# Ties for the loads of w2, h2T and w1 to products, a third output buffer, and a lower pace of the first stages, in a fused spectral-gate and MLP step

## The chip, the core and the metric

The kernel runs on one core of a Trainium2 chip. The metric is device time in microseconds, taken as the median of repeated executions. The engines are TensorE (PE, matmul), VectorE (DVE), ScalarE (ACT), GpSimd (POOL) and SyncE (SP). In this kernel SP issues nearly all loads and every transposing load, in one queue and in order; GpSimd issues nearly all stores and a few loads. Matmuls read weights and streams from the on-chip memory (SBUF) and add up in PSUM banks, from which ScalarE or VectorE take them.

## What is computed

A gated sum of two branches, and then all its gradients for a given `grad_out`. Cut to what matters:

```python
X = rfft2(x) * (w_r + 1j * w_i)                # x: 2048 x 1024
a = irfft2(X, s=(2048, 1024)).astype(bfloat16) # branch A
h = x @ w1 + b1                                # w1: 1024 x 3584
r = where(h > 0, h, 0)
b = (r * r) @ w2 + b2                          # branch B, w2: 3584 x 1024
g = sigmoid((x * gate_w).sum(-1, keepdims=True))
out = g * a + (1 - g) * b
# returned: out, and its vjp at grad_out for
# x (through both branches and the gate), w_r, w_i, w1, b1, w2, b2 and gate_w
```

The large matrix products are: h (hidden), its gradient (dh), the gradients of w2 (h transposed times the output gradient) and of w1 (x transposed times dh), the output of branch B (h times w2), and the product of dh with w1 turned (the gradient of x through B). In the kernel the output gradient already times (1-g) is `dbn`, its transpose `dbT`.

## The kernel before

One chain of products on TensorE runs from start to end, and a second, smaller chain, the two Fourier transforms, is threaded into it.

**The main chain** has three stages. `mlp_in` makes h (line 724) and its gradient (line 734) in *units* of two products each, 128 features by 512 rows, and stores the squared activations and the gradients to two scratch tensors in HBM, `h2T_scr` and `dhT_scr`. The pre-activation passes through ScalarE, the gradient through VectorE (line 738). w2 is read by transposing loads `load_w2` into `w2T`, two for each group of 512 features.

`mlp_grads` makes the gradients of w2 and w1 in 28 *blocks*. Each group of 512 features is fetched back from scratch by four transposing loads (`fetch`, line 180) into one of two tiles called "odd" and "even", and serves two blocks. A block is one level of a fast 2 x 2 multiplication: seven products `p1` to `p7` in place of eight, with sums of quarter matrices as operands. For w2 (blocks 0 to 13, lines 913 and following) the sums of the group are S1 to S4 (`left`, line 887), and those of `dbn` are T1 to T4 (`right`, lines 861 to 870), made once at the start of the stage. For w1 (blocks 14 to 27, `Turned`, line 978) the sums of x (`sums_of_x`, line 1006) are made once, and those of each group (`sums_of_group`, line 1023, G1 to G4) for every group. Products accumulate in PSUM banks `pX` and `pV`. ScalarE copies what is needed between products (line 920, `c` and `u`), VectorE adds it up (line 924, `wlo` and `whi`), and GpSimd stores the block. `p7` ends in such an addition, kept as `added`.

`mlp_out` makes branch B's output, `out`, and then the product of dh with w1. h blocks 0 and 1 (256 rows each) are done as eight full products (line 1419), the rest as blocks of seven products (line 1324). Its operands are w2 in two halves, `w2L` (in the place of `dbn`, free after block 13) and `w2R`; three large sums of them, `wT` (line 1384, 3.89 us each) must be made on VectorE before block 2's later products, and each block has its own sums `dS` (line 1320). `prepare` (lines 1241, 1242), `close` (1253, 1254, 1259) and `put` (1263) finish an output tile from `a` (branch A, from `ax_scr`), `go` (the given gradient) and the products. The quarters of w1 for the last products come by transposing loads (`quarter`), two columns of chunks at a time.

**The side chain** has four stages: the row and column transforms of x and of grad_out (`first_stage_of_x`, `first_stage_of_grad`, lines 276 and 309; each tile is fetched by `source` at line 632, folded on VectorE, and stored to `z_scr`); `fft_mid`, 32 turns over `z_scr` which transform along the rows, multiply with the filter, form the filter's gradients and transform back (products `px`, line 415, and `pv`, line 446; VectorE's result `pc`, stored to `y_scr`, lines 452 to 455); and `fft_out`, the transforms back. For a tile, `fft_out` loads rows `r` from `y_scr` on GpSimd's queue (line 225), copies and folds them on ScalarE (line 552) and VectorE (lines 557, 558, `folded`), multiplies (line 565, `rows_back`, and `columns_back`), combines on VectorE (lines 581 to 593, result `yo`) and stores `yo` to `ax_scr` (line 594).

**What sets the order.** Both chains are generators. `spread` advances the side chain by a given number of steps for each unit of the main chain. In `mlp_in` that number is `first_rate`: 2.1 steps a unit until `fft_mid` starts (the flag "mid"), 1.6 after it, none in the last six units. In `mlp_grads`, a product has weight 0.5; the rate is 0.9 a weight until the sums of x are handed on (flag "res1", after block 13's products), and from then the steps left, `todo` less those done, over 48. `fft_out` issues its first three loads of `r` and yields eight times before the first `folded`. The emitted order is then turned by a scheduler into the order on each engine; each engine runs its own instructions strictly in order. `after(ins, earlier)` adds a dependency by hand: by default a wait, or, where it says NoSync, only an order. `turn["PE"]` is the last product issued so far in the order written by hand.

**Which loads stand where.** `rows_of_w2` (line 616) loads four row blocks of one half of w2, 512 KB. In `mlp_grads` seven such loads fill `w2L`, emitted at the ends of the blocks from number 16 on; nothing but the place being free makes them wait. `load` in `mlp_out` (line 1223) fetches a block of h2T or dhT in two loads of 896 KB; block 1 goes to "odd3", a tile of its own, so nothing holds it back either. Each piece of `quarter` waits only for its destination being free. All of these stand in SP's queue with the transposing loads of the groups.

Of the kernel before, what the change touches and what calls it, by code (L numbers as in the profile page):

```python
# [10 lines left out]
P = 128  # L11
# [6 lines left out]
FDT = FP16  # L18
# [121 lines left out]
def kernel(  # L140
# [27 lines left out]
    S, D = xf.shape  # L168
# [3 lines left out]
    R1, R2 = g.R1, g.R2  # L172
    NT = S // P
    Q, H, LW, W1 = D // 4, D // 2, g.Df + 1, g.Df
# [5 lines left out]
    turned = lambda out, in_: nc.sync.dma_start(out=out, in_=in_, transpose=True)  # L180
    ld, st = nc.sync.dma_start, nc.gpsimd.dma_start
# [16 lines left out]
    pers, _ = pool("pers", stack=ctx)  # L198
    dram, _ = pool("dram", space=DRAM, stack=ctx)
# [33 lines left out]
    def after(ins, earlier, wait=mybir.DependencyClass.Sync):  # L233

        if earlier is not None:
            info = mybir.DependencyInfo(wait, mybir.DependencyReason.DATA)
            tc.add_manual_dep(ins.ins, earlier.ins.name, info, reason="paced")


    turn = {"PE": None, "DVE": None, "ACT": None}  # L240
# [288 lines left out]
    def fft_out():  # L529
        odd_p, later["odd_s"] = pool("odd3", "right")  # L530
        later["odd3"] = odd_p.tile([P, FC * 2 * P], BF16, name="odd3", tag="odd3")
        fb, fbs = pool("f3", "right")
        ki = fb.tile([P, 2, P], FDT, name="ki", tag="ki")
        ld(out=ki[:], in_=cten["ki"].ap())
        ci = fb.tile(list(consts["ci"].shape), FDT, name="ci", tag="ci")
        ld(out=ci[:], in_=cten["ci"].ap())
        tiles = [(T, i) for T in range(2) for i in range(NT)]
        r, fold, rt, evens = {}, {}, {}, {}

        def load(n):  # L540
            T, i = tiles[n]
            r[n] = fb.tile([P, D], FDT, name="r", tag="r", bufs=4)
            rows_of(st, y_scr, T, i, r[n], False)

        def folded(n):

            fold[n] = fb.tile([P, 2, 2, P], FDT, name="rf", tag="rf", bufs=2)
            rv = r[n][:].rearrange("p (c h g i) -> p c h g i", c=2, h=2, g=4)
            a, b = rv[:, :, 0, 1::2, :], rv[:, :, 1, 3::-2, ::-1]
            evens[n] = fb.tile([P, 2, 2, P], FDT, name="re", tag="re", bufs=2)  # L550
            for im in range(2):
                nc.scalar.copy(  # L552
                    out=evens[n][:, im].rearrange("p g (h i) -> p g h i", h=2),
                    in_=rv[:, im, :, 0::2, :].rearrange("p h g i -> p g h i"),
                )
            to = lambda sign: fold[n][:, sign].rearrange("p c (g i) -> p c g i", g=2)
            in_turn(V(out=to(0), in0=a, in1=b, op=ALU.add), "DVE")
            in_turn(V(out=to(1), in0=a, in1=b, op=ALU.subtract), "DVE")

        def rows_back(n):  # L560
            pk = fps.tile([P, 8, P], FP32, name="pki", tag="ps2", bufs=2)
            even = [evens[n][:, im, g_] for im, g_ in ((1, 0), (0, 0), (0, 1), (1, 1))]
            odd = [fold[n][:, sign, im] for sign, im in ((0, 0), (1, 0), (1, 1), (0, 1))]
            for b, block in enumerate(even + odd):
                in_turn(mm(pk[:, b, :], lhsT=block, rhs=ki[:, int(b in (1, 2, 4, 5)), :], start=True, stop=True), "PE")
            rt[n] = fb.tile([P, 8, P], FDT, name="rt", tag="rt", bufs=2)
            nc.scalar.copy(out=rt[n][:], in_=pk[:])

        def columns_back(n):
            T, i = tiles[n]  # L570
            pu = fps.tile([P, 2, H], FP32, name="pui", tag="ps2", bufs=2)
            column_stage(pu, rt[n], ci, turn["PE"])
            e = fb.tile([P, 2, H], FDT, name="e", tag="e", bufs=2)
            nc.scalar.copy(out=e[:, 0, :], in_=pu[:, 0, :])
            nc.scalar.copy(
                out=e[:, 1, :].rearrange("p (c d x) -> p c d x", c=2, x=2),
                in_=pu[:, 1, :].rearrange("p (c x d) -> p c d x", c=2, x=2),
            )
            ev = fb.tile([P, 2, Q], FDT, name="ev", tag="ev", bufs=2)
            A, B = (e[:, 0, o : o + Q].rearrange("p (c d) -> p c d", c=2) for o in (0, Q))  # L580
            in_turn(V(out=ev[:, :, 0:P], in0=A, in1=B, op=ALU.add), "DVE")
            evf = ev[:].rearrange("p c d -> p (c d)")
            in_turn(V(out=evf[:, Q:P:-1], in0=A[:, 0, :], in1=B[:, 0, :], op=ALU.subtract), "DVE")
            in_turn(V(out=evf[:, 2 * Q - 1 : Q + P : -1], in0=B[:, 1, 1:], in1=A[:, 1, 1:], op=ALU.subtract), "DVE")
            in_turn(nc.vector.tensor_copy(out=ev[:, :, P : P + 1], in_=e[:, 0, P::Q].rearrange("p (c o) -> p c o", o=1)), "DVE")
            tt = fb.tile([P, 2, 2, Q], FDT, name="tt", tag="tt", bufs=2)
            V(out=tt[:, 0].rearrange("p a b -> p (a b)"), in0=evf, in1=e[:, 1, :], op=ALU.add)
            V(out=tt[:, 1].rearrange("p a b -> p (a b)"), in0=evf, in1=e[:, 1, :], op=ALU.subtract)
            yo = fb.tile([P, D], FDT, name="yo", tag="yo", bufs=2)
            yv = yo[:].rearrange("p (a l) -> p a l", a=2)  # L590
            V(out=yv[:, :, 0:Q], in0=tt[:, :, 0, :], in1=tt[:, :, 1, :], op=ALU.add)
            V(out=yv[:, ::-1, H - 1 : Q : -1], in0=tt[:, :, 0, 1:Q], in1=tt[:, :, 1, 1:Q], op=ALU.subtract)
            nc.vector.tensor_copy(out=yo[:, 0::Q], in_=tt[:, :, :, 0].rearrange("p a b -> p (a b)"))
            st(out=ax_scr[T][i][:], in_=yo[:])

        load(0), load(1), load(2)
        for _ in range(8):
            yield
        folded(0)
        for n in range(len(tiles) + 1):  # L600
            if n < len(tiles):
                rows_back(n)
                yield
            if n > 0:
                columns_back(n - 1)
            if n + 3 < len(tiles):
                load(n + 3)
            if n + 1 < len(tiles):
                folded(n + 1)
            yield  # L610
        fbs.close()


    def rows_of_w2(t_, fc, half):
        src = B_w2[fc * P : (fc + 4) * P, half * H : (half + 1) * H]
        ld(out=t_[:, fc : fc + 4, :], in_=src.rearrange("(q p) e -> p q e", p=P))

    db_p, db_s = pool("db")
    dbn = db_p.tile([P, NT, D], BF16, name="dbn", tag="dbn")
# [4 lines left out]
    later = {}  # L624
# [184 lines left out]
    def mlp_grads():  # L809
# [255 lines left out]
        for k in range(2, NB // 2):  # L1065
            a = blk.pop(k - 1)
            g, second = divmod(k, 2)
            b = blk[k] = Block(k)
# [72 lines left out]
        for k in range(NB // 2 + 2, NB):  # L1141
            g, second = divmod(k, 2)
            b = Turned(k)
            b.p1()
            yield each
            b.p2()
            if second:
                fetch(g + 2, 0)
            yield each
            a.p4()  # L1150
            if not second:
                sums_of_group(g, 3, 4)
            yield each
            b.p6()
            yield each
            a.p3()
            if not second:
                fetch(g + 1, 1)
            yield each
            b.p5()  # L1160
            yield each
            b.p7()
            if second and g + 1 < len(jobs):
                sums_of_group(g + 1, 1, 2, tie=b.added)
            yield each
            n = k - NB // 2 - 2
            if n < FC // 4:
                rows_of_w2(later["w2L"], 4 * n, 0)
            a = b
        a.p4()  # L1170
        yield each
        a.p3()
# [5 lines left out]
    BW = 2 * P  # L1178
# [13 lines left out]
    def mlp_out():  # L1192
# [23 lines left out]
            after(ins, turn["DVE"], mybir.DependencyClass.NoSync)  # L1216
            turn["DVE"] = ins

        def load(which, k, issue=ld):
            t_ = later["odd" if k % 2 else "even"][:, 0 : FC * BW].rearrange("p (c b) -> p c b", b=BW)  # L1220
            v_ = (h2T_scr if which == "h" else dhT_scr)[:].rearrange("c p s -> p c s")
            for h in (lo, hi):
                issue(out=t_[:, h, :], in_=v_[:, h, k * BW : (k + 1) * BW])
            blks[which, k] = t_


# [159 lines left out]
        def quarter(view, i, j):  # L1386
            for c in range(0, KH, 2):
                f0 = (i * KH + c) * P
                turned(view[:, c : c + 2, :], B_w1[j * H : (j + 1) * H, f0 : f0 + 2 * P])
                yield  # L1390


# [15 lines left out]
        prepare(0)  # L1408
        fetch_g(1)
        made = w2_sums()  # L1410
        load("h", 1)
        for fc in range(0, FC, 4):
            rows_of_w2(cR, fc, 1)
        steps = [(0, 0), (1, 0), (2, 0), (0, 1), (1, 1), (2, 1), (3, 0), (3, 1)]
# [294 lines left out]

    def first_rate():  # L1710
        left_[0] -= 1
        return 0.0 if left_[0] < 6 else 1.6 if "mid" in later else 2.1

    for _ in spread(units, spec, first_rate):
        pass
    grads = mlp_grads()
    next(grads), next(grads)
    todo = 22 + 2 * (NT + 4) + 14 + 5 + 4 * R1 + 2 + 8 + 2 * 28

    def rate():  # L1720
        if "res1" not in later:
# [52 lines left out]
```

## Time and profile before

Thirteen executions gave a median of 1254.54 us, 1245.82 to 1264.34. One execution was profiled.

| what | us |
|---|---|
| profiled execution, its time | 1251.89 |
| its span, first to last instruction | 1250.1 |
| TensorE busy | 1196.5 |
| VectorE, ScalarE, GpSimd busy | 831.6, 619.6, 362.6 |
| first products of the two first side stages (line 276), from | 33.6 |
| `fft_mid`'s forward products (line 415), first and last start | 284.9 to 663.0 |
| last unit's products (line 734) start | 471.4 |
| gradient blocks of w2 and w1 | 474.0 to 882 |
| `fft_out`'s products (line 565), first and last start | 714.3 to 894.4 |
| full products of h blocks 0 and 1 (line 1419) | to 932 |
| blocks of seven products (line 1324), from | 932.7 |

How to read the lines of the profile in what follows. A line of a timeline gives the start, the duration in microseconds (from the first to the end of the last where several equal instructions stand together), the engine, the line of the kernel, the operation, the result and its operands, the shapes, the count and, in brackets, how long the engine sat idle before it and what released it. A line of the view of waits gives the engine and the instruction that waited, what it waited for, and then the total in microseconds, the number of waits and the longest. The row PEclk gives, for 40 slices of the span, the clock granted to TensorE in tenths of the full one, where 9 is 0.9 or more. SPq is SP's DMA queue; its duration is the time to issue, not to land.

### The profile page before, as it was taken

The page shows a single profiled execution, that of the slowest core. Times are in us where ns is not written, and L with a number is a line of the kernel's source. Part 1 is how long each engine was busy: PE and PEld are TensorE (multiplying, and loading weights), DVE is VectorE, ACT ScalarE, POOL GpSimd, SP SyncE. Part 2 cuts the span into 40 slices and gives each one's busy share as a digit, 9 for nine tenths or more (in the row PEclk, how much of TensorE's full clock was granted, in tenths as well). Part 3 has the DMA queues.
Part 4 walks back from the last instruction along what each step waited for, and adds up shares of the span by engine and source line. Part 5 has one row for each costly group of instructions (what it writes and reads, how often), then busy time and mean ns, then how long its engine had stood idle before and what let it go on. Part 6 is the DMA issues. An engine that isn't in the chain of part 4 may idle for free. (4 is left out here: it accounts for less than half of the span.)

```text
span 1250.1 us, 20093 instructions
## 1 busy us (share of the span) xinstructions
PE 1196.5 (96%) x7231; PEld 657.3 (53%) x7328; DVE 831.6 (67%) x1808; ACT 619.6 (50%) x1128; POOL 362.6 (29%) x587
## 2 busy tenths in 40 slices
PE   9999998999999998999999599999997999999997
PEld 5555554444444443444447499999543444444443
DVE  3556476768888867776788177777357665875464
ACT  4658686557777763444433166666321323233232
POOL 0124354225555532333234444653100000000000
PEclk9999999999999998999999799999998999999999
DMA  9566576575769699689979999985895558856450
GB/s 284 193 188 183 168 180 208 126 202 176 194 192 232 150 211 178 156 170 232 242 177 229 198 188 192 236 186 173 216 245 141 156 173 200 209 182 201 142 157 34
DMA packets 332382, 234.44 MB, mean 188 GB/s; under 512 B 197772, under 2 KB 291114, under 8 KB 332282
## 3 DMA queue, kind: packets, MB, share of 16 engines
q1 hardware_dynamic: 301856, 142.50, 53.0%
q0 software_dynamic: 30224, 90.61, 24.1%
q8 instruction: 57, 0.93, 0.3%
q14 instruction: 43, 0.35, 0.1%
q10 hardware_dynamic: 202, 0.04, 0.0%
HBM read 107.24 MB, written 81.81 MB: 151 GB/s over the span
## 5 line engine op out<-in xcount | busy, mean ns | idle before, releaser
L724 PE MATMUL ph<-xT,w1g 128*128 128x512 bf16 x866 | 214.8, 381 | 3.2 <-DMA w1g<-in_B_w_dram 1.2
L734 PE MATMUL pd<-dbT,w2T 128*128 128x512 bf16 x875 | 209.7, 379 | 0.9
L734 PEld LDWEIGHTS <-w2T 128*128 128x128 bf16 x896 | 87.0, 98 | 102.3 <-issue 0.3
L724 PEld LDWEIGHTS <-w1g 128*128 128x128 bf16 x896 | 85.7, 98 | 96.0 <-DMA w1g<-in_B_w_dram 1.5
L738 DVE SCALAR_TENSOR_TENSOR dhT<-pd,rT 128x512 bf16<-128x512 f32 x112 | 76.7, 686 | 77.2 <-PE pd L734 67.6
L726 ACT ACTIVATE rT<-ph,b1col 128x512 bf16<-128x512 f32 x112 | 77.5, 692 | 65.9 <-PE ph L724 65.6
L1324 PEld LDWEIGHTS <-dS 128*128 128x128 f16 x574 | 56.3, 99 | 79.7 <-DVE dS L1320 9.5
L978 PEld LDWEIGHTS <-res 128*128 128x128 bf16 (+1 forms) x896 | 86.2, 98 | 12.9 <-issue 3.0
L225 POOL DMA_DIRECT2D z_scr<-u x96 | 58.6, 616 | 100.0 <-ACT u L293 42.1
L418 ACT CAST x<-px 64x512 f16<-64x512 f32 x128 | 74.0, 578 | 19.5 <-PE px L415 18.4
L978 PEld LDWEIGHTS <-X 128*128 128x128 f16 x672 | 66.1, 100 | 23.3 <-issue 14.6
L920 ACT COPY u<-pX 128x512 f32<-128x512 f32 x56 | 32.7, 584 | 85.6 <-PE pX L913 53.6
L727 ACT ACTIVATE h2T<-rT 128x512 bf16<-128x512 bf16 x112 | 70.5, 630 | 2.1
L225 POOL DMA_DIRECT2D r<-y_scr x96 | 58.2, 612 | 39.2 <-ACT re L552 10.4
L1324 PEld LDWEIGHTS <-odd 128*128 128x128 bf16 (+1 forms) x392 | 38.4, 98 | 48.1 <-issue 2.1
L1324 PEld LDWEIGHTS <-even 128*128 128x128 bf16 (+1 forms) x392 | 38.2, 98 | 48.2 <-DMA even<-h2T_scr 2.4
L1264 POOL DMA_DIRECT2D out_dram<-ot x16 | 8.6, 540 | 176.7 <-DVE ot L1263 176.7
L913 PEld LDWEIGHTS <-S 128*128 128x128 f16 x336 | 33.1, 99 | 41.9 <-issue 1.7
L1324 PE MATMUL pX<-wT,dS 128*128 128x512 f16 x196 | 46.4, 390 | 9.0 <-DVE dS L1320 9.0
L455 POOL DMA_DIRECT2D y_scr<-pc x64 | 36.2, 567 | 56.4 <-DVE pc L452 49.9
L1345 DVE TENSOR_TENSOR cu<-pV,u 128x512 f16<-128x512 f32 x28 | 19.3, 689 | 49.0 <-PE pV L1324 39.5
L779 POOL DMA_DIRECT2D h2T_scr<-h2T x28 | 20.6, 736 | 96.5 <-ACT h2T L727 94.2
(263 smaller groups left out, 2458.9 us busy)
## 6 DMA issues: line engine op xcount, KB each, us to landing
h2T_scr<-h2T POOLq DMA_DIRECT2D x28, 512.0 KB, 4.7
dhT_scr<-dhT POOLq DMA_DIRECT2D x28, 512.0 KB, 5.3
z<-z_scr SPq DMA_DIRECT2D x64, 128.0 KB, 3.3
y_scr<-pc POOLq DMA_DIRECT2D x64, 128.0 KB, 3.5
ax_scr<-yo POOLq DMA_DIRECT2D x32, 256.0 KB, 6.2
w1g<-in_B_w_dram SPq DMA_DIRECT2D x14, 512.0 KB, 5.1
out_dram<-whi POOLq DMA_DIRECT2D x28, 256.0 KB, 5.0
out_dram<-wlo POOLq DMA_DIRECT2D x28, 256.0 KB, 6.0
```

The source lines that it names most:

```text
L225: issue(out=a, in_=b) if stored else issue(out=b, in_=a)
L418: nc.scalar.copy(out=x[lanes[n], c, :, 0:HW], in_=px[lanes[c], n])
L455: st(out=y_scr[:][c, :, :, h].rearrange("r x t l -> (r x) t l"), in_=pc[:, n])
L724: mm(ph[:], lhsT=w1g[:, dc, fc % 2 * P : (fc % 2 + 1) * P], rhs=xT[:, dc, ss], start=(dc == 0), stop=(dc == DC - 1))
L726: nc.scalar.activation(rT[:], ph[:], ACT.Relu, bias=b1col[:, fc : fc + 1])
L727: nc.scalar.activation(h2T, rT[:], ACT.Square)
L734: mm(pd[:], lhsT=w_[:, ec, fc % FGC * P : (fc % FGC + 1) * P], rhs=dbT[:, ec, ss], start=(ec == 0), stop=(ec == DC - 1),)
L738: return STT(out=dhT, in0=pd[:], scalar=2.0, in1=rT[:], op0=ALU.mult, op1=ALU.mult, accum_out=gb1part[:, fc, sb : sb + 1],)
L913: self.mm = mm(acc[:], lhsT=lhs[:, t, c_], rhs=rhs[:, t, :], start=start and t == 0, stop=t == KH - 1, skip_group_check=True,)
L920: nc.scalar.copy(out=t_[:], in_=self.X[:])
L978: ins = mm(acc[:, j * FH : (j + 1) * FH], lhsT=lhs[:, t, c_], rhs=rhs[:, t, :], start=start and first_ is None, stop=t == KH - 1, skip_gro ...
L1324: pe(mm(acc[:], lhsT=lhs[:, c, :], rhs=rhs[:, c, :], start=start and c == 0, stop=c == KH - 1, skip_group_check=True,))
```

## The change

It has six parts. (1) `yo` gets a third buffer. (2) `fft_out` yields twelve times in place of eight before its first `folded`, and `todo` counts the four. (3) The seven loads of `w2L` wait for `added`, VectorE's addition after `p7`, of blocks 16 to 22. (4) The load of h block 1 waits for `added` of the last block, kept as `later["tie"]`. (5) Every transposing load of a quarter of w1 waits for the last TensorE product issued before it in the written order. (6) `first_rate` starts with 1.75 in place of 2.1.

```diff
-            yo = fb.tile([P, D], FDT, name="yo", tag="yo", bufs=2)
+            yo = fb.tile([P, D], FDT, name="yo", tag="yo", bufs=3)
...
         load(0), load(1), load(2)
-        for _ in range(8):
+        for _ in range(12):
             yield
         folded(0)
...
-    def rows_of_w2(t_, fc, half):
+    def rows_of_w2(t_, fc, half, tie=None):
         src = B_w2[fc * P : (fc + 4) * P, half * H : (half + 1) * H]
-        ld(out=t_[:, fc : fc + 4, :], in_=src.rearrange("(q p) e -> p q e", p=P))
+        after(ld(out=t_[:, fc : fc + 4, :], in_=src.rearrange("(q p) e -> p q e", p=P)), tie)
...
             n = k - NB // 2 - 2
             if n < FC // 4:
-                rows_of_w2(later["w2L"], 4 * n, 0)
+                rows_of_w2(later["w2L"], 4 * n, 0, b.added)
             a = b
+        later["tie"] = b.added
         a.p4()
...
-        def load(which, k, issue=ld):
+        def load(which, k, issue=ld, tie=None):
...
-                issue(out=t_[:, h, :], in_=v_[:, h, k * BW : (k + 1) * BW])
+                after(issue(out=t_[:, h, :], in_=v_[:, h, k * BW : (k + 1) * BW]), tie)
...
-                turned(view[:, c : c + 2, :], B_w1[j * H : (j + 1) * H, f0 : f0 + 2 * P])
+                after(turned(view[:, c : c + 2, :], B_w1[j * H : (j + 1) * H, f0 : f0 + 2 * P]), turn["PE"])
                 yield
...
-        load("h", 1)
+        load("h", 1, tie=later["tie"])
...
-        return 0.0 if left_[0] < 6 else 1.6 if "mid" in later else 2.1
+        return 0.0 if left_[0] < 6 else 1.6 if "mid" in later else 1.75
...
-    todo = 22 + 2 * (NT + 4) + 14 + 5 + 4 * R1 + 2 + 8 + 2 * 28
+    todo = 22 + 2 * (NT + 4) + 14 + 5 + 4 * R1 + 2 + 12 + 2 * 28
```

## The prediction

> **What bounds the kernel now.** I read the busy shares first, then TensorE's waits, then each engine's timeline around the longest of them, and last the windows. The profiled execution took 1251.89 us, its span 1250.1; 1.8 us lie around it.
>
> ```profile
> PE 1196.5 (96%) x7231; PEld 657.3 (53%) x7328; DVE 831.6 (67%) x1808; ACT 619.6 (50%) x1128; POOL 362.6 (29%) x587
> PEclk9999999999999998999999799999998999999999
> ...
> PE pX L978 <- ACT c L920: 14.1, 1, 14.1
> PE pX L1324 <- DVE dS L1320: 9.0, 1, 9.0
> PE pV L913 <- DVE even L887: 3.2, 1, 3.2
> PE pk L276 <- ACT f L268: 3.1, 5, 2.1
> PE pu L309 <- ACT ft L280: 2.9, 2, 2.7
> ```
>
> TensorE (PE) is the bound: 1250.1 - 1196.5 = 53.6 us idle in all, and the change adds or removes no matmul. So it can win only idle time, and the time in which matmuls run at half clock after an idle stretch. Four such slow stretches follow the four long waits: 195.2 to 198.6, 485.3 to 492.1, 693.5 to 710.6 and 942.7 to 952.9 us. A matmul there takes twice its time, so half of the busy part is lost. These places are the whole prize.
>
> *Place A, 690 to 711.* ScalarE (ACT) runs in order, and a copy TensorE needs (`c`, L920) stands behind a copy (L552) that waits for the first rows of y:
>
> ```profile
> 682.96 0.58 ACT L953 CAST whi<-pX 128x512 bf16<-128x512 f32 x1 [1.16 <-PE pX L978]
> 702.01 0.71 ACT L552 COPY re<-r 128x256 f16<-128x256 f16 x2 [18.47 <-DMA r<-y_scr]
> ...
> 678.32 4.73 SPq L616 DMA_DIRECT2D w2L<-in_B_w_dram  x5
> 683.15 9.44 SPq L180 DMA_TRANSPOSE odd<-dhT_scr  x1
> ...
> 694.06 10.67 SPq L1223 DMA_DIRECT2D odd<-h2T_scr  x2
> ```
>
> The loads r were issued from 686.63 on and took 15 us to land (median 15.2 in 640 to 700, against 6.6 in 720 to 875). Beside them ran five 512 KB loads of w2 and two 896 KB loads of h2T. TensorE: 14.07 us idle; the matmuls after it to 710.6 lose another half of 6.1, 3.0. Place A costs 17.1.
>
> *Place B, 932 to 953.* VectorE (DVE) must finish three sums of w2 (3.89 us each) and `dS` before h block 2's third product; it stood idle first, its input `go` held up on the SP queue behind transposes of w1:
>
> ```profile
> 929.66 0.69 DVE L1242 TENSOR_TENSOR v<-na,w2L 128x1024 f16<-128x1024 f16 x1 [6.75 <-ACT na L1241]
> 933.70 1.23 DVE L1254 CUSTOM_DVE_ANT_0 ot<-cu,go 128x1024 bf16<-128x1024 f16 x1 [2.74 <-DMA go<-in_grad_out_dram]
> 939.01 3.89 DVE L1384 TENSOR_TENSOR wT<-w2L,wT 128x7168 f16<-128x7168 bf16 x1
> ...
> 896.74 27.03 SPq L180 DMA_TRANSPOSE w1q<-in_B_w_dram  x13
> 926.65 2.11 SPq L1237 DMA_DIRECT2D go<-in_grad_out_dram  x1
> ```
>
> Waits 0.60, 0.78 and 9.02, plus half of the 4.0 us (948.9 to 952.9) at half clock: 12.4.
>
> *Place C, 481 to 492.* Waits of 3.22 and 0.70 as the gradient products begin (sums T1 2.28, S3 1.66, S1 1.21 us on VectorE stand behind four instructions of the middle stage), and a half-clock stretch of 6.8 holding about 6.2 of work: 3.1. In all 7.0.
>
> *Place D, first stages.* Waits 2.12 at 119 and 2.70 at 191, each after two transposes of w2 (8.4 and 5.3 us on SP) held up a tile's source, so that VectorE waited 3.29 and 4.24 for it. Smaller waits 0.27 and 0.22, and half of 3.4 (195.2 to 198.6): 7.0 in all.
>
> **The change, part by part.** Where instructions move I compared the order of the two built programs on each engine; they give order, no times.
>
> *Slower first stages (2.1 to 1.75 side steps per unit).* Two steps a tile and about 1.86 us a unit made a tile every 4.42 us; at 2.1/1.75 that is nominally 5.3, about 4.9 over the stretch because the last units and the ends are unchanged. Sources are fetched some 2.5 tiles ahead, so the lead grows by 2.5 x 0.48 = 1.2 us. That shortens the two waits of 2.12 and 2.70 by 1.2 each and leaves the second, at 1.5, under the 2.12 that kept the clock up: 2.4 + 1.7 = 4.1. A third pair of w2's transposes now falls inside these stages and takes back one such remainder, about 1.1. Bounds: 0 and the whole 7.0; I take 3. Price: by the order, 149 side steps are done at the end of the units instead of 159 and nine more remain of the middle stage when the gradient products start.
>
> *Place C in the new order.* The sum T1 now directly follows the last instruction of the units, and the middle stage's products come after the first four gradient products. T1 can start at 474.2 instead of 478.6, 4.4 earlier; the products come earlier too, by the pair px and pv (0.87, 473.11 to 473.98) that no longer stands ahead of them. Wait left: 3.92 - 4.4 + 0.87 = 0.4, and no half clock. Gain 7.0 - 0.4 = 6.6, bounds 3 and 7. Against it: the displaced middle-stage work runs beside the sums of x in blocks 13 to 16 (2.28 each). I added the rows of one such stretch: VectorE gets about 43 us of work against TensorE's 37; before it was 22.5 against 19.1, and TensorE waited 2.65 in all. Walking the queue row by row gives five waits, together 5.3 and none over 1.6. Cost 2.7, bounds 1 and 7.
>
> *Place A.* By the same order 191 side steps instead of 200 are done when `res1` is set, so the rate for the rest rises from (275 - 200)/48 = 1.56 to (279 - 191)/48 = 1.83 steps per unit weight; four more yields stand before the first `folded`, and w2's loads wait for the seventh product of blocks 16 to 22. In the new SP order only the group's transposes, the first w2L load, and ki and ci lie near the r loads; the h2T load waits for the last block. From the last pv (before: 676.15) to what TensorE needs, the rows give: 3.0 to the store's issue, 0.6 issuing, 4.7 to landing (median there), 1.8 for three r issues, 6.6 to landing, 2.5 until `c` is out: 19.2. The product that needs it comes nine products later, 15.7 us: 3.5 us of stall left, and I put 2.5 of half-clock loss on it because 2.70 at 191 was followed by one. Gain 17.1 - 6.0 = 11.1. If r still takes 15.2 us, stall 12.1 and 3 after it: gain 2.0. If y lands in 3.5 (its median over the span) and r in 2.6 (its shortest): none left, gain 17.1. I take 6.6, since what made it 15 is moved away.
>
> The Trainium skill, TensorE: Matmul & The Clock Gate, section "What's actually happening", puts the drop to half clock after an idle window of about 3.4 us and the recovery after as much busy time. The trace differs for the first: 2.70 us at 191 sufficed, 2.12 at 119 did not, and the slow stretches lasted 3.4 to 17.1 us. By the page, place A's remaining 3.5 us would halve the clock for some 3.4 us, an estimate of 1.7 us lost in place of my 2.5, and the gain at A would be 11.9.
>
> *w2L loads spread over blocks 16 to 22.* Behind each waiting load on SP stand the next transposes of dhT, two per block. Transposes take 6 to 7.6 us (27.77 for four), a load 0.95 of issue, a block 14.7. In the old trace the queue idled 4.3 and 3.1 us before each group's fourth transpose, which landed by 784 where its sums on VectorE ran at 790. Seven loads x 0.95 fit: 0, down to -6 if each costs its issue. The cover is this slack; gone, the sums G are late and TensorE after them.
>
> ```profile
> 575.00:600.00 25.00, 24.89 (x116) 11.33 (x117) 19.47 (x36) 9.48 (x17) 9.91 (x17) 1.00 1.20 231
> 650.00:678.00 28.00, 25.59 (x181) 17.67 (x182) 27.37 (x42) 13.00 (x23) 10.99 (x16) 1.00 0.94 202
> 690.00:704.00 14.00, 0.41 (x4) 0.21 (x3) 0.49 (x3) 1.17 (x4) 2.90 (x6) 0.62 1.22 132
> 750.00:775.00 25.00, 25.00 (x268) 22.85 (x266) 18.99 (x60) 16.60 (x31) 12.46 (x21) 1.00 1.18 195
> ```
>
> (Columns: length, then busy time of PE, its weight loads, DVE, ACT, POOL; clock, DMA share, GB/s.) The DMA is as full at 575 as at 750 and moves 231 GB/s with TensorE never stalled; 3.67 MB more over 100 us is 37.
>
> *w1's quarters tied to TensorE's place.* On SP they now come one by one beside blocks 3 and 4, after the last `go` and `a` loads, where 13 stood together (27.03). Behind each waiting one stand later h and d blocks. VectorE's chain walked with its rows: `v` 922.9, T2 done 929.5, T4 933.3, store and close 935.9, `dS` sums 939.3; the product that needs it is ready at 938.15. Left 1.2. Gain 12.4 - 1.2 = 11.2; bounds 5 (if `a` is still late by the old 6.75) and 12.4. The second rows' quarters end about 1083 where their first sum is due at 1073.6 for one half and 1095 for the other; the early half ends 1072: 0, bounds -2 and 2.
>
> *Third yo buffer.* VectorE waited 6.6 us in all for a yo to be stored, at times when TensorE was full: 0.
>
> Sum: 3 + 6.6 - 2.7 + 11.1 + 11.2 = 29.2 us. 1251.9 - 29.2 = 1222.7. The profiled run lay 2.65 under the median of 13 runs, 1254.54, so the forecast for the median is 1225.
>
> **Rivals.** *R1, place A stays.* TensorE's 14 us were r's latency, and if that comes from the r loads' own scattered 64 KB packets and not from the loads beside them, it remains 15: gain 2.0 instead of 11.1, 1234. For it: DMA share was 1.22 at 132 GB/s, so bytes were not the limit. Against: 25 later loads of the same shape took 6.6. *R2, slower: the SP queue becomes the bound.* Two transposes (14.6) plus a load's issue (0.95) and its 512 KB at 195 GB/s (2.7) are 18.2 against 14.7 a block; seven blocks slip 24.5, and four groups with half-clock losses of 3 add 12: 1225 + 36 = 1261. It decides once the slip per group passes the slack of 4.3 and 3.1. For it: DMA share above 1 from 725 to 825. Against: 231 GB/s at 575. The Trainium skill, DMA: Bandwidth & Descriptors, section "Latency and other measured facts", gives transposes 261 GB/s, an estimate of 8 us for a group's 2 MB; the trace's 27.77 denies it, and by the page R2 could not happen. *R3, it doesn't do what it says.* The tie orders issue, but VectorE's three sums start as late as before because `a`, not `go`, was last (6.75 for `na`): B's 11.2 are not won, 1236, and with A as in R1 1245. For it: VectorE idled 6.75 for `na` ahead of 2.74 for `go`. Against: `na` is made by ScalarE from `a` (L1241), whose load stood behind the same 13 transposes and landed after 923.87.
>
> **How the numbers follow.** Forecast 0.55 (own range 1215 to 1234), R1 0.22, R3 0.11, R2 0.12. About 0.5% (6 us) is what a measurement of this kernel tells from no change: faster means under 1248.3. Forecast, R1 and most of R3 (0.08 of 0.11) lie below it; R2 in part, slipping on two groups only, ends near no change (0.04 of 0.12): faster 0.85, same 0.07, slower 0.08. The range reaches from 1213 (A, C and D won whole: 6.0 + 0.4 + 4.0 better, and near 2 for the spread of runs) to 1245 past R1 and R3, leaving out R2 and a little.
>
> **What would show it.** Right: no wait over 4 us of L978 on `c`; r landing near 7 us; T1 right after the last unit; waits on `dS` under 2; clock near 1.0 from 925 to 975. Wrong: waits of L978 on `G` or on transposes in blocks 18 to 27 (R2), r at 15 us (R1), VectorE idle for `na` before 930 (R3), or VectorE-caused waits over 7 us in blocks 13 to 16.

## The result, and where the time went

The changed kernel takes 1238.11 us (median of 11 runs, 1233.31 to 1245.33) against 1254.39 for the kernel before (48 runs): a ratio of 0.9887, 95% interval 0.9862 to 0.9912. It is faster, by 16.3 us between the medians; the forecast was 29 less. In all that follows the ratios leave out executions that were disturbed as a whole (one of e18 took 3086 us), and the profiled ones of e3 and e4 were such, so of those two only the order of issue and waits that other runs show too are read. The profiled execution of the changed kernel has a span of 1233.8 us against 1250.1, so the 16.3 us between them can be read as the whole of the difference.

The page of the changed kernel, its busy times and the granted clock by slices:

```profile
PE 1195.4 (97%) x7231; PEld 657.3 (53%) x7328; DVE 831.0 (67%) x1808; ACT 622.9 (50%) x1128; POOL 362.2 (29%) x587
PEclk9999999999999999999999989999999999999999
```

The work is the same, and TensorE is still the bound; its idle time fell from 53.6 to 38.4. Its waits, as the view of waits of the changed kernel has them (total, number, longest):

```profile
PE pX L978 <- ACT u L920: 6.4, 1, 6.4
PE pv L446 <- DVE y L439: 3.3, 5, 1.3
PE pX L913 <- DVE S L887: 3.2, 1, 3.2
PE pV L913 <- DVE wlo L924: 2.7, 1, 2.7
PE pX L1325 <- DVE dS L1321: 2.4, 1, 2.4
PE pV L978 <- DVE wlo L924: 2.3, 1, 2.3
```

The waits of 14.1 and 9.0 are gone, and so are both of the first stages. But place A keeps 6.4, place C has a wait of the same size as before on another sum, and three lines (y, and wlo twice) are waits that the kernel before had only in pieces of at most 1.4. TensorE's timeline of the changed kernel shows where, and which of them were followed by half clock (8 matmuls of this size take 1.9 us, 16 short ones 1.9; 3.3 to 3.6 is half clock):

```profile
477.81 3.28 PE L913 MATMUL pX<-T,S 128*128 128x512 f16 x8 [3.17 <-DVE S L887]
...
637.56 3.52 PE L913 MATMUL pV<-dbn,even 128*128 128x512 bf16 x8 [2.73 <-DVE wlo L924]
...
661.07 0.38 PE L446 MATMUL pv<-y,ab 128*128 128x512 f16 x1 [1.31 <-DVE y L439]
...
685.70 3.43 PE L978 MATMUL pV<-even,res 128*128 128x256 bf16 x16 [2.26 <-DVE wlo L924]
...
715.52 3.57 PE L978 MATMUL pX<-even,X 128*128 128x256 f16 x16 [6.42 <-ACT u L920]
```

Place by place, waits plus what half clock took (for the changed kernel, half of the time in which matmuls ran at half clock: a stretch of 3.4 us filled with matmuls costs 1.7):

| place | before | changed | gain | forecast |
|---|---|---|---|---|
| D, first stages (121, 191) | 7.0 | 0 | 7.0 | 3 |
| C, start of the gradient products | 7.0 | 3.17 + 0.60 + 1.4 = 5.2 | 1.8 | 6.6 |
| blocks 12 to 16 (630 to 693) | 2.65 | 2.73 + 1.7 + 3.28 + 2.26 + 1.6 = 11.6 | -8.9 | -2.7 |
| A | 17.1 | 6.42 + 2.0 = 8.4 | 8.7 | 11.1 |
| B | 12.4 | 2.41 + 1.7 = 4.1 | 8.3 | 11.2 |
| sum | | | 16.9 | 29.2 |

(3.28 is the sum of the five waits of pv. TensorE's idle time outside these places is 17.2 us before and 17.5 after.) Two causes of the shortfall are on VectorE's timeline of the changed kernel:

```profile
474.33 2.29 DVE L864 TENSOR_TENSOR T<-dbn,T 128x4096 f16<-128x4096 bf16 x1 [3.31 <-DMA h2T_scr<-h2T]
...
634.00 1.23 DVE L1023 TENSOR_TENSOR G<-odd 128x2048 f16<-128x2048 bf16 x1 [7.39 <-DMA odd<-dhT_scr]
```

At 471 VectorE had T1, S3 and S1 done, as forecast, and then stood at T2 for the last *store of h2T*: T2's tile lies where the units' buffers lay. At 626 it stood 7.39 us for a transposed group, with `wlo` behind it and TensorE behind `wlo`. The four transposes of that group landed in 5.5 to 13.9 us, in e1 (below) in 4.4 to 7.0; in the changed kernel loads of the filter for the middle stage stand among them on SP (617 to 624), in e1 these had gone at 592. That the displaced loads held the transposes up is likely by this, not shown. The third is place A, on ScalarE:

```profile
707.86 0.41 ACT L552 COPY re<-r 128x256 f16<-128x256 f16 x1 [6.88 <-DMA r<-y_scr]
712.63 0.41 ACT L552 COPY re<-r 128x256 f16<-128x256 f16 x1 [4.37 <-DMA r<-y_scr]
712.94 0.58 ACT L953 CAST whi<-pX 128x512 bf16<-128x512 f32 x1
714.27 0.71 ACT L552 COPY re<-r 128x256 f16<-128x256 f16 x2 [0.75 <-issue]
714.89 0.58 ACT L920 COPY u<-pX 128x512 f32<-128x512 f32 x1
```

The same picture as before, with the last pv starting at 693.0 in place of 675.8: the copy `u` stands behind copies that wait for r.

### The profile page after: what moved, and what is told of

The parts are those of the page before. It is cut to its first block, busy times and chain, and to the rows that moved or that the text cites. A ratio compares the mean times of both kernels' runs of the same rounds, so it can differ in the third digit from the quotient of the medians.

```text
span 1233.8 us, 20101 instructions
## 1 busy us (share of the span) xinstructions
PE 1195.4 (97%) x7231; PEld 657.3 (53%) x7328; DVE 831.0 (67%) x1808; ACT 622.9 (50%) x1128; POOL 362.2 (29%) x587
## 5 line engine op out<-in xcount | busy, mean ns | idle before, releaser
L978 PEld LDWEIGHTS <-res 128*128 128x128 bf16 (+1 forms) x896 | 87.3, 99 | 16.5 <-issue 5.1
L978 PEld LDWEIGHTS <-X 128*128 128x128 f16 x672 | 65.3, 99 | 17.1 <-issue 8.8
```

The lines of the kernel that those rows point to most:

```text
L978: ins = mm(acc[:, j * FH : (j + 1) * FH], lhsT=lhs[:, t, c_], rhs=rhs[:, t, :], start=start and first_ is None, stop=t == KH - 1, skip_gro ...
```

## The experiments

Ratios are to the kernel before on the same chip, with their 95% intervals.

**e1: the pace alone undone.** `else 1.75` back to `else 2.1`, everything else as changed.

> The changed kernel with first_rate back at 2.1. Theory (the pace): the two waits on the first stages' tiles come back, about 6.8 us with the half-clock stretch, but ten more side steps are done before the gradient products, so the wait of 2.73 at 637 and the waits of about 3 between 660 and 686 shrink by 2 to 4 us: about 1241. Rival (the pace has no price later; the new waits at 637 to 686 come from the other edits): all of them stay, 1245.

1228.12 us, 0.9826 (0.9788 to 0.9864): *faster* than the full change (0.9887), where both expectations had it slower. The first stages' waits came back, and all that was new between 630 and 693 went, and most of place A:

```profile
121.07 0.62 PE L276 MATMUL pk<-kf,f 128*128 128x128 f16 x8 [2.25 <-ACT f L268]
194.70 0.74 PE L309 MATMUL pu<-cf,ft 128*128 128x256 f16 x8 [3.63 <-ACT ft L280]
486.79 1.90 PE L913 MATMUL pV<-T,even 128*128 128x512 f16 x8 [3.22 <-DVE even L887]
692.63 2.72 PE L978 MATMUL pX<-G,X 128*128 128x256 f16 x16 [2.38 <-ACT c L920]
```

The slower pace saves about 7 us in the first stages and costs more later: it leaves nine more steps of the middle stage to the blocks where VectorE also makes the sums of x. The two profiled executions lie 5.3 us apart (1228.5 and 1233.8); the rest of the 10 us between the medians is not read from a trace.

**e2: eight yields and 8 in `todo`.**

> The changed kernel with eight yields before the first folded and 8 in todo. Theory (TensorE waits there for the rows of y as long as the work put between does not cover their way): four steps less are 4 / 1.75 = 2.3 weights or about 4.6 products of 1.75 us, 8 us of cover; the wait of 6.42 grows to about 14, time about 1246. Rival (the loads that were moved away were the cause of place A): the wait stays near 6, 1238.

1234.71, 0.9892 (0.9858 to 0.9925), and a wait of 6.05 at place A for 6.42. The cover theory fell: the copies of `folded` kept nearly their place on ScalarE's queue, one position apart, and 14.0 us of products stood between the last pv and the stalled product, where the changed kernel has 15.7.

**e3: no ties on w2L and h block 1.** (`rows_of_w2(..., 0)`, `load("h", 1)`.)

> The changed kernel without the ties of the seven w2L loads and of h block 1. Rival of the run before (contention): with 3.7 MB of w2L and 1.8 MB of h2T beside them the r loads take 15 us and more again, the wait of 6.42 grows by 4 or more: 1243 to 1248. Theory (cover): the r loads take 10 to 12 us with or without them, 1236 to 1240.

1237.77, 0.989 (0.9855 to 0.9925): no difference from the full change. Two of the loads went out at 662, three at 675 and two at 685, before the first r at 706: at this pace they are out before it.

**e4: no tie on w1's quarters.**

> The changed kernel without the tie of w1's quarters to TensorE's place. Theory: 13 transposes stand together on SP again before the inputs of the third and fourth output tile, the wait on dS at 934 grows from 2.4 to about 9, and with the two DMA waits about 8 us are lost: 1246. Rival (place B's gain came from earlier loads of w2L and h block 1): stays at 1238.

0.9972 (0.992 to 1.0024), against 0.9887 with the tie; the median of all executions is 1253.91. By the ratios the tie is worth some 10 us of the whole. The wait on `dS` is 9.0 again, as in the kernel before and in e10:

```profile
PE pX L1325 <- DVE dS L1321: 9.0, 1, 9.0
```

**e7: the tile of x moved** behind the sums, so that T2 lies where nothing is stored from:

```diff
-        xr = wb.tile([P, NT, D], BF16, name="res1", tag="res1")
         sb, sbs = pool("m2s")
+        rb, rbs = pool("m2r")
+        xr = rb.tile([P, NT, D], BF16, name="res1", tag="res1")
```

> The changed kernel with the tile of x (res1) laid behind the sums, so that the sum T2 no longer lies on the buffers of h2T and does not wait for their last store. Theory (place C now hangs on that store, which lands 9 us after its issue): T2 starts at 471 instead of 474.3, TensorE's wait of 3.17 and its half-clock stretch fall below 1: 4 to 5 us less, about 1234. Rival (the transposes of h2T or VectorE's own queue take the store's place): the wait stays at 2 or more, 1237 to 1239.

1233.77, 0.9826 (0.9755 to 0.9897), span 1227.0. In its timeline of VectorE T2 follows S1 at once, and TensorE has no wait between 465 and 488:

```profile
469.74 1.21 DVE L888 TENSOR_TENSOR even<-even 128x2048 f16<-128x2048 bf16 x1
470.87 2.28 DVE L865 TENSOR_TENSOR T<-dbn,T 128x4096 f16<-128x4096 bf16 x1
```

**e8: pace at 2.1 and no ties on w2L and h block 1.**

> The changed kernel with first_rate at 2.1 and without the ties of w2L and h block 1. Theory (the ties and the pace do the same work at place A: at 2.1 the r loads meet the w2L and h2T loads unless these are tied; at 1.75 they come 18 us later anyway): r lands in 15 us again, TensorE waits 12 to 14 at place A, time 12 to 15 above the run with 2.1 and ties, about 1241. Rival (the ties are worth nothing, as at 1.75): 1228, wait near 2.4.

1240.87, 0.9877 (0.98 to 0.9954), against 0.9826 with the ties. First the view of waits, then the view of the tile r, for the loads issued from 682 to 692 (issue to landing, minimum, median, maximum):

```profile
PE pX L978 <- ACT c L920: 15.8, 1, 15.8
```

```profile
DMA to landing us min/median/max: 10.2/15.7/16.1
```

In e1, with the ties, the r loads issued in that time landed in 3.4/7.0/7.6. At this pace the ties take 13 us off the wait; at 1.75 (e3) they do nothing. No run separates the w2L loads from that of h block 1.

**e9: pace at 2.1, eight yields, two yo buffers**, so that the three ties alone remain.

> The changed kernel with first_rate at 2.1, eight yields and two yo buffers, so that only the three ties remain of the change. Theory (the order on ScalarE is the same with 8 and 12 yields; the third buffer never held TensorE): 1228, as with them. Rival (the four yields hide part of place A at this pace): the wait of 2.4 grows by up to 8, 1232 to 1238.

1240.71, 0.991 (0.9873 to 0.9947). Place A is at 1.14 (2.38 in e1), so neither the yields nor the third buffer are needed there; but TensorE waits 8.5 us in all between 805 and 847, where e1 has 2.5.

**e10: the pace alone done**, on the kernel before.

> The kernel before with nothing but first_rate at 1.75. Theory (the pace moves the last rows of y some 18 us later, past the w2L loads): place D won (7), place A down to a wait of 6 to 7 and a half-clock stretch (7 won), new waits of 4 to 7 between 637 and 686, place B as before: 1254 minus 8 to 10, about 1245. Rival (without the ties place A stays at 14): about 1252.

1243.08, 0.9915 (0.9879 to 0.9951). Its waits: place B and all the new ones are there, and place A is at 6.0 without any tie.

```profile
PE pX L1324 <- DVE dS L1320: 9.0, 1, 9.0
PE pX L978 <- ACT u L920: 6.2, 2, 6.0
PE pX L913 <- DVE S L887: 4.1, 1, 4.1
PE pv L446 <- DVE y L439: 4.0, 5, 1.8
```

The r loads issued from 697 to 712 landed here in 6.6 (median), and the wait is still 6.0. So slow r loads are not all that can hold place A: the first of them went out only 6.0 us after the last store of y was issued (3.4 in the changed kernel), and 14.0 us of products stood between the last pv and the stalled product.

**e12: pace at 2.1, sources two tiles further ahead** (six `src` buffers, `xs[i + 5]` for `xs[i + 3]`, `xs[n + 2]` for `xs[n]`).

> The changed kernel with first_rate at 2.1 and the first stages' sources fetched two tiles further ahead (six buffers in place of four). Theory (place D is the lead over the transposes of w2, whatever gives it): the waits of 2.3 and 3.6 at 121 and 195 fall to nothing without a slower pace, 6 to 7 us less than with 2.1 alone, about 1221. Rival (the loads are issued earlier but stand behind the same transposes): waits as before, 1228.

1222.74, 0.9761 (0.9682 to 0.984). Half each: the wait at 121 is gone, the one at 192 is still 3.52. ScalarE's timeline shows that a source was not what it waited for:

```profile
190.10 0.37 ACT L292 CAST u<-pu 128x256 f16<-128x256 f32 x1 [5.09 <-DMA z_scr<-u]
190.37 0.48 ACT L293 ACTIVATE u<-pu,flip 128x256 f16<-128x256 f32 x1
190.74 1.01 ACT L280 CAST ft<-pk 128x1024 f16<-128x1024 f32 x1
```

**e13: e12 with res1 moved and no side steps in the last seven units** (for six).

> All that the runs point to, on the changed kernel: first_rate at 2.1 but none in the last seven units (T1 directly behind the last unit on VectorE), sources two tiles further ahead, res1 laid behind the sums. From the run with 2.1 (1228): less 6 to 7 (place D), less 4 to 5 (place C) gives 1216 to 1219 if both places are what the runs so far say; 1228 if place A takes back what they give.

1223.07, 0.9754 (0.9701 to 0.9807). Place C is at 0.67 and A at 0.68, yet it gains nothing over e12 that can be measured: its profiled execution has waits of 7.2 us between 819 and 839.

**e14: pace at 2.1 and two yo buffers.**

> The changed kernel with first_rate at 2.1 and two yo buffers. In the run with two buffers and eight yields TensorE waited 8.5 us in all between 805 and 847, with three and twelve 2.5. Theory (the third buffer took these): they are back, 1234 to 1240. Rival (the yields or the order on the queues did): 2 to 3 us of waits there, 1228.

1232.39, 0.9837 (0.9747 to 0.9927); 0.93 us of waits between 805 and 847. The third buffer alone is not seen to matter.

**e15: pace at 2.1, none in the last seven units.**

> The changed kernel with first_rate at 2.1 and none in the last seven units, res1 where it was. Theory (T1 early is worth little as long as T2 lies on a buffer of h2T): TensorE waits 3 us or more on the sum S2 at place C, about 1227. Rival (the store has landed by then at this pace): wait below 1, 1223.

1226.29, 0.9782 (0.9711 to 0.9853). No wait at place C but 0.7 on a small transpose (L848): T1 directly follows the last unit, and T2 at 481.37, 5.8 us after the store's issue at 475.53, did not wait for it. So the rival was right: at this pace the store had landed within 5.8 us, where in the changed kernel T2 was released 9.2 us after the store's issue (465.10 to 474.33). Why it took longer there stays open; the same four transposes started beside it in both.

**e16: e12 with four u buffers** for two.

> The run with 2.1 and sources further ahead, and four buffers for u in place of two. Theory (ScalarE waits there for u's store to z_scr, 5 us, and TensorE for ScalarE): the wait of 3.5 at 192 and its half-clock stretch go, 3.5 + 1.7 = 5 us less, about 1218. Rival (something behind it, the stores' own queue or the next source, takes its place): 2 us or more stay, 1221 to 1223.

1215.67, 0.9686 (0.9623 to 0.975). Nothing over 0.3 is left between 34 and 476. Its waits begin with

```profile
PE pV L917 <- DVE even L891: 3.2, 1, 3.2
PE pX L1329 <- DVE dS L1325: 2.4, 1, 2.4
PE pV L982 <- DVE wlo L928: 2.1, 3, 1.4
```

**e17: e13 with four u buffers.**

> The combined kernel with four u buffers. If the store of u is the cause, its wait of 4.69 at 193 and the half-clock stretch go: 1223 less 6, about 1217. If not, 1221 to 1224.

1216.12, 0.9706 (0.9633 to 0.9779). These two are the fastest, and cannot be told apart. Both beat the changed kernel.

**e18: pace at 2.1, eight yields, three yo buffers.**

> The changed kernel with first_rate at 2.1 and eight yields, three yo buffers. Theory (the yields act later, through the rate and the order of the transforms back beside blocks 22 to 25): waits of some 8 us between 805 and 847 as in the run with two buffers, about 1234. Rival (only both together do it): 1 to 3 us there, about 1228. Place A is expected near 1 to 2.5 in either case.

1243.17, 0.9894 (0.9826 to 0.9963), where e1 has 1228.12, 0.9826; the intervals overlap. In its profile one wait does it, on VectorE and from there on TensorE; the timeline of VectorE:

```profile
816.99 1.23 DVE L1023 TENSOR_TENSOR G<-even,G 128x2048 f16<-128x2048 bf16 x1 [4.61 <-DMA even<-dhT_scr]
```

TensorE waits 5.24 for it at 818 and half clock follows, to 823.7. It is a group's transposing load that landed late, with a w2L load issued on SP just ahead of it. e1 shows the same wait with 1.41, the changed kernel with 0.76. That the yields do this through the higher rate is argued, not shown. e9 against e14 is the same pair with two yo buffers: 1240.71 and 1232.39. So at 2.1 eight yields came out slower in both pairs, by 15 and 8 us, neither clear of its interval; at 1.75 (e2) they did not.

## Why the prediction was wrong, step by step

The sign, the four places and what ties them were right; the size was not. It put 29 us of gain, and measured are 16. By the table, place D came out 4.0 better than forecast, and C 4.8, the blocks 12 to 16 6.2, A 2.4 and B 2.9 worse.

*The slower pace was the step that failed.* It was priced as 3 us won in the first stages and 2.7 lost in blocks 13 to 16. Measured are 7.0 won and 8.9 lost in blocks 12 to 16: a loss of 1.9 where a gain of 0.3 was put. The prediction walked VectorE's queue through the sums of x and found "five waits, together 5.3 and none over 1.6"; the profile has the five waits of pv (3.28 together) and two more, 2.73 and 2.26, each with half clock after it (1.7 and 1.6). One of them is not VectorE's work at all but a late transpose (7.39 at 634), which the walk could not contain. e1 shows it as a whole: without the slower pace the kernel takes 1228 in place of 1238, and between 630 and 693 only the 2.1 on `wlo` of the kernel before are left.

*Place A: a size, and a dependence that was not seen.* The path from the last pv was worked out as 19.2 us under 15.7 of cover. The cover was right (15.7, from the end of the last pv); the path took 22.1, since the r loads landed in 10.5 (median; 6.2 to 11.8), not 6.6, beside three transposes that took 14.4 to land. From the first r's issue to the copy that waits last, 11.7 us went by where the sum had 8.4; that the transposes did it is argued. The half-clock loss of 2.5 was right in the main (2.0). "I take 6.6, since what made it 15 is moved away" holds at pace 2.1, where r landed in 7.0 and the wait was 2.4. What the forecast missed is that two parts of the change do the same work: the slower pace moves r past the w2L loads by itself (e10: 6.0 without ties), and then the ties buy nothing (e3). At 2.1 they buy 13 us (e8 against e1). Rival R1 had the effect, a longer r, but for another reason, and its doubt that the loads beside r were the cause is answered by e8: at 2.1 they are.

*Place C: a wait behind the wait.* Forecast 0.4 us left, measured 5.2. The order of instructions was as forecast and the first sums ended on time; T2 then waited for a store. The kernel before had that dependence too, hidden: its T2 started only at 484.1, 10.9 us after the store's issue at 473.2, and waited for nothing:

```profile
484.13 2.48 DVE L864 TENSOR_TENSOR T<-dbn,T 128x4096 f16<-128x4096 bf16 x1
```

e7 takes the dependence away, and of place C 0.7 is left. The walk added VectorE's durations and asked nothing of the tiles' former users.

*Place D: right in sign, under half the size, and with half of the cause for one of its two waits.* The wait at 121 is a late source (e12). The prediction took the one at 192 for the same. In the kernel before a source was late there too, but ScalarE stood as long for the store of u, two tiles back, and was released 0.3 us later:

```profile
191.91 0.42 DVE L255 TENSOR_TENSOR uv<-src 128x512 f16<-128x512 bf16 x1 [4.24 <-DMA src<-in_grad_out_dram]
192.19 0.37 ACT L292 CAST u<-pu 128x256 f16<-128x256 f32 x1 [4.25 <-DMA z_scr<-u]
```

With the source early the wait stayed (e12, 3.52); with four u buffers besides it went (e16).

*Place B: right, 8.3 of 11.2.* VectorE's chain from the third `v` to `dS` took 16.5 us, as worked out (16.4); `v` itself came 1.1 later for TensorE's place, because of `na`. So 2.41 was left for 1.2, and half clock followed with 1.7. The mechanism, `go` and `a` held behind 13 transposes, is shown by e4. R3 had its sign in small, VectorE idle for `na` 2.69 and 1.12 where it was 6.75 before, but not its price.

*Nothing for the w2L loads in blocks 16 to 22, the quarters' second rows and the buffer* held for the changed kernel within 1 us; R2's slip did not come. That it is near is shown by e18. The yields, priced at place A alone, take nothing off the wait there (with eight it is 6.05 in e2 for 6.42, 1.14 in e9 for 2.6 in e14, 1.2 in e18 for 2.38 in e1).

## What to carry to other kernels

When a change slows one stage to spare it a stall, follow the work that is left over to the stage that will take it, and look there for a resource already full; here it cost more than it saved, while two more buffers on the loads and on the stores won the stall without it. When a wait is removed by order, look up for each next instruction who last used its tile, and whether that user is a store still under way. And parts that cure the same stall do not add: price each with the others in place.

## What was not expected of the hardware

Half clock did not follow the length of the idle stretch. The same product after the same wait ran at full clock in e1 (the line at 486.79 above: 8 matmuls in 1.90 us after 3.22 idle) and at half clock in e16:

```profile
476.90 3.59 PE L917 MATMUL pV<-T,even 128*128 128x512 f16 x8 [3.23 <-DVE even L891]
```

2.26 us sufficed in the changed kernel at 685.70. What the clock followed can be read from the trace's records of the granted clock. All half-clock stretches between 30 us and the last 20 us of the 17 profiled executions last 3.41 us or a multiple of it (in the kernel before 3.41, 6.83, 17.07 and 10.24), and within an execution they all begin on one grid of that step. What counted was TensorE's idle time inside one cell of the grid:

| run, product at | idle before it, us | idle in the fullest cell, us | clock in the cell after it |
|---|---|---|---|
| before, 121.46 | 2.12 | 1.60 | full |
| e1, 486.79 | 3.22 | 1.77 | full |
| changed, 685.70 | 2.26 | 2.01 | half |
| e16, 476.90 | 3.23 | 2.02 | half |
| before, 193.89 | 2.70 | 2.63 | half |

In these executions every cell with 2.01 us of idle or more was followed by a cell at half clock, and none that was itself at full clock and held 1.79 or less was; between the two both occur. So a wait of 2 to 3.5 us costs up to 1.7 us more or nothing, according to where it falls on the grid. The Trainium skill, TensorE: Matmul & The Clock Gate, section "What's actually happening", speaks of a free-running window of about 3.4 us, and the grid agrees with it; it gives the drop after at least one idle window, and here the measurement decides: 2.01 us of idle in a window sufficed.
